# Three FFN1 tiles begun inside the attention of batch 0, and attention visits of three tiles throughout

## The chip, the cores and the metric

One NeuronCore of a Trainium2 chip runs the whole program; the other cores are idle. The metric is the device time of one execution in microseconds. The profiler gives the span from the first to the last instruction; in the executions listed below the time is the span plus 1.8 us. Where the text calls an execution slow, it is slower than its fellows. Batches, quads (groups of four heads; quad n belongs to batch n div 3) and FFN tiles are numbered from 0.

## The reference, cut to what matters

```python
# q, k, v: 8 batches x 12 heads x 448 x 64
scores = q @ k.T / sqrt(64) - log(448)
attn   = 1 / (1 + exp(-scores)) @ v          # sigmoid attention, no row sums
x      = attn.transpose(0, 2, 1, 3).reshape(3584, 768)
g      = x @ w_gate                          # 768 x 1536
out    = (g * sigmoid(g) * (x @ w_val)) @ w_out
```

A head needs no softmax sum, so TensorE and ScalarE (the sigmoid) can be interleaved freely with the FFN of an earlier batch.

## The kernel before

Attention of batch 0 runs first. After that the FFN of batch b is the main stream, and the attention of later batches is worked into it in "visits": a few QK tiles between two FFN units. A quad has seven QK tiles (`chunk(n, c)` or `qk_tile` + `sig_tile`), then one PV of 28 small matmuls. All PSUM is a ring of four tiles of two banks; every QK tile, PV, transposition, FFN1 tile and FFN2 tile takes the next one in turn and waits for its last user's readers. In the rows of the traces `pt` is the output of a sigmoid of the attention, `xT` the attention's result and FFN1's input (six tiles for a batch, one for each pair of heads), `hT` what FFN1's gate writes, and `T` a transposed q or k.

```python
ring = [psD.tile([128, 2, 512], FP32, ...) for i in range(4)]
class Banked:                       # takes the next tile of the ring
    def __init__(self, user=None):
        k = ring_at[0] % 4
        ring_at[0] += 1
        self.t = ring[k]
        ...
def qk_tile(n, c):                  # 4 matmuls of 64x64, 448 columns
    sc = Banked().t ...
def sig_tile(n, c, sc):             # ScalarE, 128 x 896
    nc.scalar.activation(out=pt, in_=sc[:, :, :S], func=SIGM, ...)
def pv(n, two=False):               # 28 matmuls, then 4 casts PSUM -> xT (VectorE)
    P = Banked().t ...
def ffn1(b, f):                     # 6 gate + 6 val matmuls, then the "gate":
    ...                             # ScalarE sigmoid, VectorE multiply, VectorE multiply
def ffn2(pb, m): ...                # 24 matmuls, then 2 copies

visits = [[(n, c) for c in cs] for n in range(NJ, NQ) for cs in (range(4), range(4, C))]
...
def attn_step(group, pvs):
    for part in (group[:2], group[2:]):
        scs = [(n, c, qk_tile(n, c)) for n, c in part]
        while pvs:
            pv(pvs.pop(0))
        for n, c, sc in scs:
            sig_tile(n, c, sc)
```

At the end of batch 0 two FFN1 tiles are begun while PV(2) is still to come: their first four input pairs (eight matmuls) need only PV(0) and PV(1).

```python
early = []
for f in range(2):
    Df = Banked("f")
    ffn1_mm(Df, 0, f, range(NP - 2))      # pairs 0..3
    early.append(Df)
    if f == 0:
        pv(2, two=True)
for f, Df in enumerate(early):
    ffn1_mm(Df, 0, f, range(NP - 2, NP))  # pairs 4, 5
    ffn1_gate(Df, 0, f)
```

## Time and profile before

| | before |
|---|---|
| median time of the first 3 runs | 434.53 us (434.45 to 435.88) |
| profiled execution | span 434.4 us, time 436.19 us, mean granted clock 0.995 |
| TensorE busy | 97% of the span |
| VectorE, ScalarE busy | 51%, 48% |
| visit of four QK tiles with PV | 2.48 us |
| visit of three QK tiles | 0.78 us |

The rows that the prediction rests on are printed in the prediction.

### The profile page before, as it was taken

How to read it: one execution, taken by the hardware profiler on the slowest of the kernel's cores; microseconds unless marked ns; L12 is line 12 of the kernel's file. 1: busy time of each engine (PE TensorE's matmuls, PEld its weight loads, DVE VectorE, ACT ScalarE, POOL GpSimd, SP SyncE). 2: the span in 40 equal slices, each digit the busy share in tenths (PEclk: the TensorE clock that was granted, in tenths of full speed). 3: DMA queues.
4: the chain of work that ended last, by engine and by line, in shares of the span. 5: the costliest groups of instructions: out<-in, count | busy, mean ns of one | idle time of the engine just before them, and what ended most of it. 6: DMA issues, size and time to landing. Idle time of an engine off the chain costs nothing.

```text
span 434.4 us, 7926 instructions
## 1 busy us (share of the span) xinstructions
PE 419.4 (97%) x3275; PEld 221.0 (51%) x3275; DVE 220.8 (51%) x366; ACT 208.0 (48%) x269; POOL 116.5 (27%) x166
## 2 busy tenths in 40 slices
PE   7789999999999999999999999999999999999995
PEld 2444554445555444544555544544555545555563
DVE  3645656546424656546424546555624456555322
ACT  3975885744523745745524545646533442222000
POOL 4563340730526455000426434400022100000000
PEclk9989999999999999999999999999999999999999
DMA  8999899999476997300386999720023400000234
GB/s 297 235 277 204 195 173 159 181 229 152 86 208 150 223 205 208 70 0 2 50 208 155 210 131 236 161 43 2 2 72 78 106 0 2 1 2 0 50 96 109
DMA packets 55940, 53.92 MB, mean 124 GB/s; under 512 B 33824, under 2 KB 50592, under 8 KB 55904
## 3 DMA queue, kind: packets, MB, share of 16 engines
q0 software_dynamic: 20896, 39.20, 41.7%
q1 hardware_dynamic: 34656, 13.67, 19.1%
q10 hardware_dynamic: 352, 0.56, 0.4%
q8 instruction: 25, 0.41, 0.4%
q14 instruction: 11, 0.09, 0.1%
HBM read 47.19 MB, written 11.01 MB: 134 GB/s over the span
## 4 chain that ended last, share of the span: by engine, by line
PE 81%; ACT 9%; DVE 6%; issue 3%; DMA 1%; DVEq 0%; ACTq 0%
PE ps_D L242 47%; PE ps_D L281 26%; ACT pt L202 7%; PE ps_D L191 5%; PE ps_D L214 2%; DVE hT L262 2%; DVE t L258 2%; DVE T L175 1%; DMA st<-in_q_dram 1%; DVE xT L229 1%; ACT s L256 1%; PE ps_D L167 1%; DVE c L145 0%; DVE oe L304 0%; ACT oe L300 0%
## 5 line engine op out<-in xcount | busy, mean ns | idle before, releaser
L202 ACT ACTIVATE pt<-ps_D,sb_t 128x896 f16<-128x896 f32 x168 | 156.3, 1007 | 93.4 <-PE ps_D L191 92.3
L242 PE MATMUL ps_D<-xT,wg 128*128 128x448 f16 x576 | 125.1, 353 | 2.0 <-ACT pt L202 0.4
L242 PE MATMUL ps_D<-xT,wv 128*128 128x448 f16 x576 | 125.0, 352 | 0.0
L281 PE MATMUL ps_D<-wo,hT 128*128 128x384 f16 x672 | 111.7, 326 | 0.8 <-ACT pt L202 0.4
L258 DVE TENSOR_TENSOR t<-ps_D,s 128x448 f16<-128x448 f32 x96 | 59.8, 623 | 87.9 <-ACT s L256 86.5
L256 ACT ACTIVATE s<-ps_D 128x448 f16<-128x448 f32 x96 | 52.5, 547 | 98.2 <-PE ps_D L242 96.8
L281 PEld LDWEIGHTS <-hT 128*128 128x128 f16 x672 | 65.2, 98 | 47.1 <-issue 4.6
L242 PEld LDWEIGHTS <-wg 128*128 128x128 f16 x576 | 54.8, 98 | 59.3 <-issue 11.6
L242 PEld LDWEIGHTS <-wv 128*128 128x128 f16 x576 | 56.4, 98 | 52.6
L229 DVE CAST xT<-ps_D 64x448 f16<-64x448 f32 x94 | 58.5, 622 | 29.5 <-PE ps_D L214 25.6
L311 DVE TENSOR_SCALAR osb<-ps_D 128x384 f32<-128x384 f32 x55 | 30.7, 558 | 71.5 <-PE ps_D L281 70.7
L262 DVE SCALAR_TENSOR_TENSOR hT<-ps_D,t 128x448 f16<-128x448 f32 x96 | 60.0, 625 | 10.4 <-DVE t L258 0.5
L321 POOL DMA_DIRECT2D out_dram<-osb x42 | 22.3, 536 | 143.6 <-DVE osb L311 143.6
L145 POOL CAST c<-st 128x896 bf16<-128x896 f32 x41 | 38.0, 936 | 75.6 <-issue 30.6
L191 PE MATMUL ps_D<-T,T 64*64 64x448 bf16 x672 | 48.1, 371 | 4.6 <-DVE T L175 1.9
L214 PE MATMUL ps_D<-pt,v 64*64 64x448 f16 x672 | 37.0, 357 | 0.5 <-ACT pt L202 0.5
L191 PEld LDWEIGHTS <-T 64*64 64x64 bf16 x672 | 16.3, 108 | 27.9 <-issue 19.3
L214 PEld LDWEIGHTS <-v 64*64 64x64 f16 x672 | 20.3, 109 | 13.8 <-issue 2.1
L136 POOL DMA_DIRECT2D v<-in_v_dram x24 | 17.7, 737 | 0.1
L131 POOL DMA_DIRECT2D st<-in_k_dram x20 | 14.7, 734 | 3.0 <-DVE c L145 3.0
L131 POOL DMA_DIRECT2D st<-in_q_dram x20 | 14.6, 732 | 0.6 <-DMA v<-in_v_dram 0.6
L300 ACT ACTIVATE oe<-ps_D 64x384 f32<-64x384 f32 x1 | 0.5, 484 | 27.9 <-PE ps_D L281 27.9
(21 smaller groups left out, 47.9 us busy)
## 6 DMA issues: line engine op xcount, KB each, us to landing
st<-in_q_dram POOLq DMA_DIRECT2D x20, 448.0 KB, 4.8
st<-in_k_dram POOLq DMA_DIRECT2D x20, 448.0 KB, 6.8
out_dram<-osb POOLq DMA_DIRECT2D x42, 192.0 KB, 3.1
v<-in_v_dram POOLq DMA_DIRECT2D x24, 224.0 KB, 8.0
wg<-in_moe_w_gate_dram POOLq DMA_DIRECT2D x4, 576.0 KB, 14.4
wv<-in_moe_w_val_dram POOLq DMA_DIRECT2D x4, 576.0 KB, 14.6
wo<-in_moe_w_out_dram POOLq DMA_DIRECT2D x4, 576.0 KB, 12.0
out_dram<-osb SPq DMA_DIRECT2D x12, 192.0 KB, 2.7
```

Source lines behind the costliest of these rows:

```text
L131: (eng or nc.sync).dma_start(out=st, in_=src_of(n, which))
L145: eng.tensor_copy(out=t.rearrange("p c h d -> p h c d"), in_=st.rearrange("p h (c d) -> p h c d", c=C)[:, :, lo:hi, :],)
L191: nc.tensor.matmul(out=sc[w * 64:(w + 1) * 64, h2, :S], lhsT=kt[r, w * 64:(w + 1) * 64], rhs=qt[r, :, w * 64:(w + 1) * 64], start=True, st ...
L202: nc.scalar.activation(out=pt, in_=sc[:, :, :S], func=SIGM, bias=sb_t, scale=qkscale)
L214: nc.tensor.matmul(out=P[h2 * 64:(h2 + 1) * 64, w, :S], lhsT=vt[r, h2, c * D:(c + 1) * D], rhs=pt[r, h2, :], start=(c == 0), stop=(c == C ...
L229: cp = nc.vector.tensor_copy(out=o, in_=i)
L242: nc.tensor.matmul(out=D.t[:, i, :S], lhsT=w16[f // FW][:, pr, cs], rhs=xT[(b, pr)], start=(pr == 0), stop=(pr == NP - 1),),
L256: D.read(nc.scalar.activation(out=s16, in_=D.t[:, 0, :S], func=SIGM), 0)
L258: D.read(nc.vector.tensor_tensor(out=t1, in0=D.t[:, 0, :S], in1=s16, op=MULT), 0)
L262: nc.vector.scalar_tensor_tensor(out=hT[(b // 2, f)][:, b % 2, :], in0=D.t[:, 1, :S], scalar=HSC, in1=t1, op0=MULT, op1=MULT),
L281: nc.tensor.matmul(out=D.t[:, half, :hw], lhsT=h[:, m * 128:(m + 1) * 128], rhs=wo16[f // FW][:, f % FW, half * hw:(half + 1) * hw], start ...
L311: nc.vector.tensor_scalar(out=osb[:, hs], in0=D.t[:, half, :hw], scalar1=HREC, scalar2=None, op0=MULT),
```

## The change

It wants to fill the attention of batch 0, where ScalarE sets the pace, with one more FFN1 tile, and to make the visits fit the ring: three QK tiles and a PV are four PSUM tiles.

```diff
 class Banked:
-    def __init__(self, user=None):
-        k = ring_at[0] % 4
-        ring_at[0] += 1
+    def __init__(self, user=None, at=None):      # 'at' chooses a ring place
+        if at is None:
+            at = ring_at[0] % 4
+            ring_at[0] += 1
+        k = ring_order[at]
 ...
-    visits = [[(n, c) for c in cs] for n in range(NJ, NQ) for cs in (range(4), range(4, C))]
+    tiles = [(n, c) for n in range(NJ, NQ) for c in range(C)]
+    visits = [tiles[i:i + 3] for i in range(0, len(tiles), 3)]
         if b == 1:
-            vtime.append(3 * FU1 + frac * (FIRST - 3 * FU1))
+            vtime.append(4 * FU1 + frac * (FIRST + 1.0 - 4 * FU1))
         else:
-            vtime.append(FIRST + 1.0 + (b - 2 + frac) * PER)
+            vtime.append(FIRST + 3.5 + (b - 2 + frac) * PER)
 ...  # casts of quad 3 right after those of quad 2; trans_pe(3) ahead of quad 2's QK tiles
+    chunk(2, 3)
+    chunk(2, 4)
+    k0 = ring_at[0] % 4
+    early = [Banked("f")]
+    for prs in (range(2), range(2, NP - 2)):
+        ffn1_mm(early[0], 0, 0, prs)
+    chunk(2, 5)
+    chunk(2, 6)
+    early.append(Banked("f"))
+    ffn1_mm(early[1], 0, 1, range(NP - 2))
+    pv(2, two=True, at=(k0 + 1) % 4)
+    early.append(Banked("f", at=(k0 + 2) % 4))
+    ffn1_mm(early[2], 0, 2, range(NP - 2))
     for f, Df in enumerate(early):
         ffn1_mm(Df, 0, f, range(NP - 2, NP))
         ffn1_gate(Df, 0, f)
+    ring_order[:] = [(k0 + 1 - i) % 4 for i in range(4)]
 ...  # the transpositions, loads and casts hung to a visit are now hung to a QK tile;
 ...  # 'while' over due visits became 'if': at most one visit per FFN unit
```

More of the change, by code (lines that the diff above doesn't have):

```diff
@@ L70 @@
     ring = [psD.tile([128, 2, 512], FP32, tag=f"D{i}", name=f"ps_D{i}") for i in range(4)]
+    ring_order = [0, 1, 2, 3]
     ring_at = [0]
@@ L203, in sig_tile, with pv @@
         pts[(n, c)] = pt
-    def pv(n, two=False):
+    def pv(n, two=False, at=None):
         b, j = divmod(n, NJ)
-        P = Banked().t
+        P = Banked(at=at).t
         vt = v16.pop(n)
@@ L331 @@
             for f in range(NF):
-                if (b, f) not in ((0, 0), (0, 1)):
+                if b or f > 2:
                     units.append((FU1, ffn1, (b, f)))
@@ L408 @@
     cast(2, 1, V)
+    cast(3, 0, V)
+    cast(3, 1, V)
     chunk(0, 5)
@@ L416 @@
     trans_pe(2)
-    cast(3, 0, V)
-    cast(3, 1, V)
     w_load("g", 1)
@@ L426 @@
     chunk(1, 6)
+    trans_pe(3)
     for c in range(3):
@@ L429 @@
     pv(1)
-    chunk(2, 3)
-    trans_pe(3)
     ready(4)
@@ L436 @@
     w_load("v", 3)
-    for c in range(4, C):
-        chunk(2, c)
-    early = []
-    for f in range(2):
-        Df = Banked("f")
-        ffn1_mm(Df, 0, f, range(NP - 2))
-        early.append(Df)
-        if f == 0:
-            pv(2, two=True)
+    chunk(2, 3)
[11 more added lines that the diff above has]
+    ffn1_mm(early[2], 0, 2, range(NP - 2))
     for f, Df in enumerate(early):
@@ L448 @@
         ffn1_gate(Df, 0, f)
-    begin = {(n, i): [] for n in range(NJ, NQ) for i in range(2)}
-    begin[(3, 1)] += [lambda: ready(5)]
-    begin[(4, 0)] += [lambda: fetch(6)]
-    begin[(4, 1)] += [lambda: ready(6)]
+    ring_order[:] = [(k0 + 1 - i) % 4 for i in range(4)]
+    ring_at[0] = 0
+    post = []
+    begin = {(n, c): [] for n in range(NJ, NQ) for c in (0, 4)}
+    begin[(3, 0)] += [lambda: post.append(4)]
+    begin[(3, 4)] += [lambda: ready(5)]
+    begin[(4, 0)] += [lambda: post.append(5), lambda: fetch(6)]
+    begin[(4, 4)] += [lambda: ready(6)]
     begin[(5, 0)] += [lambda: fetch(7)]
+    begin[(5, 4)] += [lambda: post.append(6)]
     begin[(6, 0)] += [lambda: ready(7), lambda: fetch(8)]
     begin[(7, 0)] += [lambda: ready(8), lambda: fetch(9)]
-    begin[(7, 1)] += [lambda: fetch(10)]
+    begin[(7, 4)] += [lambda: fetch(10)]
     begin[(8, 0)] += [lambda: ready(9), lambda: ready(10), lambda: fetch(11)]
-    for i, at in enumerate(((5, 1), (6, 1), (7, 0), (7, 1))):
+    for i, at in enumerate(((5, 4), (6, 4), (7, 0), (7, 4))):
         begin[at].append(lambda i=i: w_load("o", i))
@@ L466 @@
             begin[(n, 0)].append(lambda n=n: fetch(n + 3))
-    tcur = 2 * FU1
+    tcur = 3 * FU1
     vi = 0
-    pend, post = [], []
+    pend = []
     for dur, fn, args in units:
-        while vi < len(visits) and tcur >= vtime[vi]:
+        if vi < len(visits) and tcur >= vtime[vi]:
             group = visits[vi]
@@ L477 @@
             attn_step(group, pvs)
-            n, c = group[-1]
-            for act in begin[(n, int(c == C - 1))]:
-                act()
-            if c == C - 1:
-                pend.append(n)
-            elif n + 1 < NPE:
-                post.append(n + 1)
+            for n, c in group:
+                for act in begin.get((n, c), ()):
+                    act()
+                if c == C - 1:
+                    pend.append(n)
         if pend and (
```

## The prediction

> **What bounds the kernel now.** I read the page first (busy shares, the slices), then the waits of TensorE, then its timeline from end to end, because a group mean of 353 ns says nothing of the spacing.
>
> ```profile
> PE 419.4 (97%) x3275; PEld 221.0 (51%) x3275; DVE 220.8 (51%) x366; ACT 208.0 (48%) x269; POOL 116.5 (27%) x166
> ...
> PEclk9989999999999999999999999999999999999999
> ```
>
> TensorE is busy 97% of the span and no other engine is over half. But starts in the timeline show that matmuls overlap: six FFN1 matmuls take 1.135 us start to start (0.189 us each), a QK tile of four 64x64 matmuls 0.19, a PV of 28 takes 1.33, a transpose 0.062. I took (next start minus own start) minus these costs for every row. The excess is about 12 us before the first FFN1 tile at 28 us, 3.3 us between 36.5 and 69.2, some 10 us in the attention visits from there to 356 us, and nothing after. So three regions matter.
>
> Region one is the attention of batch 0, where ScalarE sets the pace: 21 sigmoids of 0.92 to 1.0 us run from 8.4 to 29.8 us, while TensorE has little to do and waits for buffers. These are rows of the whole timeline:
>
> ```profile
> 20.86 1.33 PE L191 MATMUL ps_D<-T,T 64*64 64x448 bf16 x12 [0.62 <-DVE T L175]
> 22.12 2.56 PE L214 MATMUL ps_D<-pt,v 64*64 64x448 f16 x28
> 24.80 2.53 DVE L229 CAST xT<-ps_D 64x448 f16<-64x448 f32 x4 [2.93 <-ACT pt L202]
> 24.81 0.95 PE L167 MATMUL ps_D<-idn,c 128*128 128x128 bf16 x14
> 27.39 0.57 PE L191 MATMUL ps_D<-T,T 64*64 64x448 bf16 x8 [1.31 <-DVE xT L229]
> 27.88 1.91 ACT L202 ACTIVATE pt<-ps_D,sb_t 128x896 f16<-128x896 f32 x2 [0.68 <-PE ps_D L191]
> ```
>
> The last two QK tiles of batch 0 need the PSUM tile that PV(1) used and wait 1.31 us until VectorE has taken PV(1) out; ScalarE is idle 0.68 us for them. PV(1) took 2.4 us where the others take 1.3: the windows view gives the clock there.
>
> ```profile
> 21.00:22.00 1.00, 1.00 (x12) 0.50 1.15 389
> 22.00:23.00 1.00, 1.00 (x16) 0.50 1.03 421
> 23.00:24.00 1.00, 1.00 (x20) 0.50 1.09 263
> ```
>
> Columns: stretch, its length, TensorE busy, granted clock, DMA share, GB/s. The clock is half from about 20.9 to 24.3 us.
>
> Region three is the visits: groups of QK tiles between FFN units. Two of them in TensorE's timeline, first with a PV, then without:
>
> ```profile
> 66.84 0.57 PE L191 MATMUL ps_D<-T,T 64*64 64x448 bf16 x8
> 67.24 1.49 PE L214 MATMUL ps_D<-pt,v 64*64 64x448 f16 x28
> 68.56 0.55 PE L191 MATMUL ps_D<-T,T 64*64 64x448 bf16 x8
> ...
> 173.11 0.76 PE L191 MATMUL ps_D<-T,T 64*64 64x448 bf16 x12
> 173.80 1.31 PE L242 MATMUL ps_D<-xT,wg 128*128 128x448 f16 x6
> ```
>
> FFN1's stream before them ends at 66.75 and 173.02 (last half begun plus 1.135), and FFN1 resumes at 69.23 and 173.80: the four-tile visit with PV costs 2.48 us, the three-tile one 0.78. Pure streaming would be 2.09 and 0.57. Both lose about 0.21 around the change of tile shape (0.09 going in, 0.12 coming out); the four-tile visit loses 0.18 more, because with PV it takes five of the four PSUM tiles, so its fifth user and the FFN1 after it wait for the first and second sigmoid (ScalarE starts them at 67.27, the second ends at about 69.13).
>
> **What the Trainium skill says.** "TensorEngine Tiling (Array Packing)", Key Properties: changing the tiling mode drains TensorE. The trace agrees: 0.09 + 0.12 us at each visit; so more visits cost more drains. "TensorE: Matmul & The Clock Gate", Part 1: the clock falls to half when a free-running window of about 3.4 us saw too little matmul activity, and the phase varies from run to run. The 3.4 us at 0.50 above fit that. "VectorE: DVE Perf Modes", the perf-mode tier table: a tensor_tensor with a PSUM operand has only the slowest mode. The trace has 623 ns for it and 622 for each fp32 cast of xT out of PSUM, so a PV leaves four casts, 2.53 us in a row. "Perfetto Trace Analysis", Identifying the Most-Contended Engine, warns that matmul busy share is a bad measure of headroom; hence my use of starts.
>
> **The change part by part.** No arithmetic is added or removed, only moved. I read the new instruction order and the PSUM tile of each step, and laid it down with the durations above.
>
> A. Batch 0. Quad 3's casts go to VectorE right after quad 2's, at 14.8 us (its loads land near 12.9; VectorE is idle then) and its transposes go to TensorE at 20.06, where it waits 0.62 us for quad 2's copies. QK(2,0..2) follow from 20.95, held by the sigmoids of their tiles' last users, to 22.2; PV(1) starts at about 22.25 as now. Then QK(2,3), (2,4), the first third of FFN1 tile 0, and QK(2,5), (2,6) after PV(1)'s casts.
> With full clock: PV(1) ends 23.57, its casts end 26.1; FFN1 tile 0 runs to 26.7, waiting for the fourth cast; QK(2,5), (2,6) to 27.1; last sigmoid ends 28.8 (now 29.8); tile 1's four pairs end 28.6, PV(2) 29.95, tile 2's four pairs 31.46, and the last two pairs of three tiles, 12 x 0.189 = 2.27, end at 33.7. Now the third tile ends at 36.5: gain 2.8 us.
> With the clock at half until 24.3: PV(1) ends 24.7, the casts 27.4, QK(2,6) 28.4, PV(2) 31.25, third tile 35.05: gain 1.45 us.
> Quad 3's transposes put 0.87 us of matmul into the window of 17.5 to 20.9 us, which had only about 1.5 us; I give 0.6 to the full clock.
>
> B. Batch 1 now has seven visits, one before each of FFN1 tiles 4 to 10, where there were six, with two transposes directly between FFN1 and a visit. Walking them, with sigmoids of 0.93, gates of two times 0.62 after a 0.55 sigmoid, and copies of 0.55: from the end of tile 2 to the end of tile 11 takes 32.6 us, of which 29.7 is streaming (9 FFN1 tiles 20.4, 21 QK 4.0, two PV 2.7, three transposes 2.6), 1.5 drains and about 1.4 waits for gates and copies. Before, the same work runs from 36.5 to 71.5 less one visit of quad 6 (2.48): 32.5. Even: -0.1 us.
> But the visit with PV(5) is shifted one unit later: in the new order PV(5) stands one QK tile ahead of batch 1's first FFN1 tile, which needs its xT; before, FFN1 tile 11 of batch 0 lay between. Casts begin 0.23 us after PV(5) ends and take 2.53, so the last xT comes at 2.76. FFN1 starts at about 0.3 and its sixth matmul is due at 1.25. TensorE waits 1.5 us, once. -1.5 us.
>
> C. Quads 6 to 23. Before: 18 pairs of visits at 2.48 + 0.78 = 3.26, 58.7 us. After: 42 visits of three at 0.78 and 18 PV at 1.33, 56.7 us, because three tiles and PV are just four PSUM tiles and nobody waits for a sigmoid. +2.0 us (3.1 from waits gone, less about 1.2 for six more visits' drains).
>
> The tail from 356 us is the same. Sum: 2.8 - 0.1 - 1.5 + 2.0 = 3.2 us with full clock, 1.9 with the half clock; weighted 2.7. From 434.5 that is 431.8; I take 431.6, as the walk of A leaves some slack that I counted in full.
>
> **The rivals.** (1) The gain of A is lost to waits in the denser batch 1: seven visits one FFN1 tile apart, with ScalarE at 3 x 0.93 + 0.55 = 3.3 us per visit against about 3.9 for TensorE. For it: the gates lag sigmoids there, and before had 0.44 to 0.64 us of excess at such visits. Against: ScalarE is not the longer one. It would give 433 to 434.5. (2) PV(5) does not stall FFN1, or batch 0 gains more: 429.5 to 430.3. Against: matmuls with pairs 4 and 5 carry waits on VectorE in the built order. (3) Weights come late: FFN1's first val weights land near 22 us in the trace, 2.5 us ahead of need; the second group's near 31.6, needed near 34.9. If the new loads of quad 5, issued some 3 us earlier, slowed them, 1 to 2 us would go. (4) The new clock window falls elsewhere and halves a dense FFN1 stretch: up to 1.7 us lost. (5) Three-tile visits with PV still wait, for the gate of the FFN1 tile just before, as the third QK takes its buffer: 18 x 0.2 = 3.6 us at most. Against: that gate ends some 0.9 us after its tile, and the third QK comes 1.7 us after.
>
> **Range and chances.** All large terms are small against 2% (8.7 us). Two clock states and the rivals span 429.6 to 433.6. Over 2% faster would need three times my sum: 0.03. Slower over 2%: 0.02.
>
> **What would show it right or wrong.** A: the last sigmoid of batch 0 ends near 28.8 and the third FFN1 tile near 33.7 (35.05 at half clock); the windows between 20 and 25 us show whether the clock fell. B: a wait of the first FFN1 tile of batch 1 on the xT casts, about 1.5 us in total, in TensorE's waits. C: visits with PV near 2.1 us instead of 2.48, those without at 0.78. I am wrong if PV visits stay at 2.4, if batch 1's visits lose over 0.4 us each, or if a weight load holds TensorE.

## More of the kernel before

The profiled execution was slower than each of the three runs. The trace of the kernel before is therefore a trace of a slow execution.

## The result, and the profile after

The changed kernel took 434.35 us (median of 6, 434.0 to 435.1) against 434.77 us (median of 6, 434.15 to 435.88) for the kernel before on the same chip. The ratio is 0.999 with a 95% interval of 0.9973 to 1.0006. (Ratios are the mean time of one kernel's fast runs over that of the other's of the same rounds, so not quite the ratio of the medians.) No difference clear of noise, where I had predicted 2.9 us.

The two traces, however, differ by 1.1 us (span 433.3 against 434.4). Where that comes from, region by region, taken from the starts of TensorE's rows in both traces:

| Stretch | before | after | gain |
|---|---|---|---|
| A: start of PV(0) to the end of the third FFN1 tile | 20.95 | 19.05 | +1.90 |
| B: from there to the end of batch 0's last FFN1 tile, without quad 6's visit | 32.61 | 33.32 | -0.71 |
| first FFN1 tile of batch 1 | 2.27 | 3.86 | -1.59 |
| C: quad 6's visits with PV(5) and on to PV(23), same work | | | +1.58 |

The last row is worked out so. From the end of that FFN1 tile to PV(23) it is 281.80 us before and 282.80 after, but the second contains one FFN1 tile (2.27) and one QK tile (0.19) more: 1.46 gained. The visit with PV(5) takes 2.48 before and 2.17 with one QK tile less after: 0.12 more. The sum of the rows is 1.18, and PV(0) starts 0.07 later in the trace after (15.53 instead of 15.46); the last FFN2 stream starts 1.12 us earlier (401.31 instead of 402.43), so the rows leave nothing over.

First the lines of region A after (times in us from the span's start, duration, engine, source line, tiles, count, idle time before and its releaser):

```profile
20.26 0.96 PE L170 MATMUL ps_D<-idn,c 128*128 128x128 bf16 x14
22.39 1.52 PE L217 MATMUL ps_D<-pt,v 64*64 64x448 f16 x28
23.95 2.55 DVE L232 CAST xT<-ps_D 64x448 f16<-64x448 f32 x4 [1.87 <-PE ps_D L217]
24.89 0.54 PE L245 MATMUL ps_D<-xT,wg 128*128 128x448 f16 x2 [0.51 <-ACT pt L205]
26.56 0.35 PE L245 MATMUL ps_D<-xT,wg 128*128 128x448 f16 x1 [0.56 <-DVE xT L232]
27.21 0.57 PE L194 MATMUL ps_D<-T,T 64*64 64x448 bf16 x8
27.70 1.90 ACT L205 ACTIVATE pt<-ps_D,sb_t 128x896 f16<-128x896 f32 x2 [1.06 <-issue]
```

PV(1) is at full speed (1.33 us to the next row's start), and the windows view confirms it: columns as in the prediction, the granted clock is the fifth figure.

```profile
21.00:22.00 1.00, 0.72 (x12) 1.00 1.17 388
22.00:23.00 1.00, 0.80 (x20) 1.00 1.02 406
23.00:24.00 1.00, 1.00 (x25) 1.00 1.11 279
```

Still, the last two sigmoids of batch 0 end at 29.6, not at 28.8 as I had them. The first FFN1 tile stops for the fourth cast of PV(1), ending at 26.5, and stands ahead of QK(2,5) and QK(2,6) in TensorE's order, so ScalarE is now idle for 1.06 us before their sigmoids. (That it waits for these tiles follows from the order and the times; the bracket says "issue", so the profile names no releaser.)

Then the first FFN1 tile of batch 1 in the trace after, in TensorE's timeline, and three rows of the list of waits (total, times, longest). The first row holds this tile's two waits, 0.30 and 0.95, and the 0.56 of batch 0's first tile; the others are waits for a gate in batch 1's visits:

```profile
68.04 0.57 PE L194 MATMUL ps_D<-T,T 64*64 64x448 bf16 x8
68.45 1.49 PE L217 MATMUL ps_D<-pt,v 64*64 64x448 f16 x28
69.77 0.36 PE L194 MATMUL ps_D<-T,T 64*64 64x448 bf16 x4
70.06 0.93 PE L245 MATMUL ps_D<-xT,wg 128*128 128x448 f16 x4
71.30 0.35 PE L245 MATMUL ps_D<-xT,wg 128*128 128x448 f16 x1 [0.30 <-DVE xT L232]
```

```profile
PE ps_D L245 <- DVE xT L232: 1.8, 3, 0.9
...
PE ps_D L217 <- DVE hT L265: 0.7, 1, 0.7
...
PE ps_D L194 <- DVE hT L265: 0.4, 1, 0.4
```

In the timeline four matmuls run, the fifth waits for the xT of pair 4 and the sixth, at 72.59, for that of pair 5. VectorE casts from 69.99 to 72.54.

A visit with PV further on shows what part C does. Compare it with the four-tile visit in the prediction:

```profile
88.00 1.30 PE L245 MATMUL ps_D<-xT,wv 128*128 128x448 f16 x6
89.23 0.57 PE L194 MATMUL ps_D<-T,T 64*64 64x448 bf16 x8
89.63 1.50 PE L217 MATMUL ps_D<-pt,v 64*64 64x448 f16 x28
90.95 0.36 PE L194 MATMUL ps_D<-T,T 64*64 64x448 bf16 x4
91.24 1.31 PE L245 MATMUL ps_D<-xT,wg 128*128 128x448 f16 x6
```

FFN1's stream ends at 88.00 + 1.135 = 89.13 and resumes at 91.24: 2.11 us. Nothing waits for a sigmoid.

So of the predicted mechanisms the trace shows the stall and the cheaper visits, at nearly the sizes given. What doesn't fit is the total: the traces differ by 1.1 us, the medians by 0.4.

### The profile page after: what moved, and what is told of

It reads as the page before. It is cut to its first block, busy times and chain, and to the rows that moved or that the text cites. A ratio compares the mean times of both kernels' runs of the same rounds, so it can differ in the third digit from the quotient of the medians.

```text
span 433.3 us, 7921 instructions
## 1 busy us (share of the span) xinstructions
PE 418.9 (97%) x3275; PEld 218.1 (50%) x3275; DVE 220.6 (51%) x366; ACT 209.9 (48%) x269; POOL 116.4 (27%) x166
## 4 chain that ended last, share of the span: by engine, by line
PE 91%; DVE 4%; ACT 3%; DMA 1%; issue 1%; DVEq 0%; ACTq 0%
PE ps_D L245 49%; PE ps_D L284 26%; PE ps_D L194 8%; PE ps_D L217 7%; ACT pt L205 2%; DVE xT L232 2%; DMA st<-in_q_dram 1%; PE ps_D L170 1%; DVE T L178 1%; DVE t L261 1%; DVE hT L265 1%; ACT s L259 0%; DVE c L148 0%; DVE oe L307 0%; ACT oe L303 0%
## 5 line engine op out<-in xcount | busy, mean ns | idle before, releaser
L245 PEld LDWEIGHTS <-wg 128*128 128x128 f16 x576 | 53.5, 98 | 59.6 <-issue 14.0
L314 DVE TENSOR_SCALAR osb<-ps_D 128x384 f32<-128x384 f32 x55 | 30.6, 557 | 72.9 <-PE ps_D L284 72.7
L217 PE MATMUL ps_D<-pt,v 64*64 64x448 f16 x672 | 36.0, 350 | 1.2 <-DVE hT L265 0.7
## 6 DMA issues: line engine op xcount, KB each, us to landing
wo<-in_moe_w_out_dram POOLq DMA_DIRECT2D x4, 576.0 KB, 15.3
```

Source lines behind the costliest of these rows:

```text
L217: nc.tensor.matmul(out=P[h2 * 64:(h2 + 1) * 64, w, :S], lhsT=vt[r, h2, c * D:(c + 1) * D], rhs=pt[r, h2, :], start=(c == 0), stop=(c == C ...
L245: nc.tensor.matmul(out=D.t[:, i, :S], lhsT=w16[f // FW][:, pr, cs], rhs=xT[(b, pr)], start=(pr == 0), stop=(pr == NP - 1),),
L314: nc.vector.tensor_scalar(out=osb[:, hs], in0=D.t[:, half, :hw], scalar1=HREC, scalar2=None, op0=MULT),
```

## The experiments

Theory 1: the trace of the kernel before was an untypical execution. It contains a stretch at half clock on the path (20.9 to 24.3 us), its time of 436.19 is 1.4 us over the kernel's median, and much of A's gain is the absence of that stretch, which most executions of the kernel before don't have either. Rival 2: the half clock belongs to the kernel before, and the change removes it. The other runs take the parts of the change apart. All kernels gave the right result. The medians come from six executions each, the kernel before has eleven in each of the three series. The series ran on different chips (the kernel before has medians of 435.21, 435.13 and 434.78 there), so two variants of different series are compared through their ratios to the kernel before, or region by region in their traces.

### before_copy: the kernel before again

No edit.

> The kernel before, unchanged, as a second look. Theory 1 (my baseline trace was an atypical execution: a stretch at half clock from 20.9 to 24.3 us cost it about 1.4 us, and time less span is 1.8 us, so that the median of 434.8 belongs to a span near 433.0): most executions have spans of 432.5 to 433.5, and a trace without half clock in 20 to 25 us ends batch 0's second FFN1 tile near 32.7 instead of 34.1. Rival 2 (the half clock is the rule for this kernel): spans near 434.4 with clock 0.995 in most executions, and the trace shows the half clock at about 21 to 24 us again.

Measured: 434.65 us (434.31 to 436.06), ratio 0.9991 (0.9965 to 1.0017); the profiled execution has a span of 432.6 us. Its windows and timeline:

```profile
10.00:12.00 2.00, 1.89 (x18) 0.58 1.05 371
12.00:14.00 2.00, 2.00 (x22) 0.57 1.29 206
20.00:21.00 1.00, 0.76 (x12) 1.00 1.29 208
21.00:22.00 1.00, 0.66 (x16) 1.00 1.14 412
22.00:23.00 1.00, 1.00 (x24) 1.00 1.03 414
23.00:24.00 1.00, 0.91 (x18) 1.00 1.12 247
```

```profile
21.34 1.52 PE L214 MATMUL ps_D<-pt,v 64*64 64x448 f16 x28 [0.50 <-ACT pt L202]
22.97 2.52 DVE L229 CAST xT<-ps_D 64x448 f16<-64x448 f32 x4 [1.88 <-PE ps_D L214]
25.55 0.57 PE L191 MATMUL ps_D<-T,T 64*64 64x448 bf16 x8 [1.13 <-DVE xT L229]
26.04 1.91 ACT L202 ACTIVATE pt<-ps_D,sb_t 128x896 f16<-128x896 f32 x2 [0.26 <-PE ps_D L191]
```

The same program has its half-clock stretch at 10 to 14 us here, where ScalarE's chain is not held up by it (ScalarE is busy all of these 4 us), and none at 21 to 24. The second early tile ends at 32.3 (34.1 in the first trace). Region A takes 14.67 to 34.57, 19.90 us instead of 20.95. So 1.05 us of A's 1.90 is the half clock of one execution, and theory 1 holds; the kernel before has no fixed half clock for the change to remove. All traces together say so more firmly. Of the five with the old batch 0 only the first has half clock on the way from PV(0) to the third tile's end, beyond a remnant at its start: A takes 20.95 there, 20.14 in visits_from_quad6, whose half clock ends at 15.4, and 19.89 to 19.90 in the other three. Of the nine with the new batch 0 eight take 19.04 or 19.05, and pv5_earlier, where the half clock ends at 15.3, takes 19.35. A is worth 0.85 us.

Against this second trace the table's sum is 0.85 - 0.71 - 1.59 + 1.58, which is 0.1 us. From PV(0) to the last FFN2 stream the whole stretch takes 385.94 us in it and 385.78 after. The other 0.79 us between the two traces of the kernel before lie ahead of PV(0), which starts at 15.46 and at 14.67. The executions agree if they are sorted by the granted clock listed with each (my sorting, after the fact). At 1.000 the kernel before has a median of 435.21 (nine executions) and the changed one 435.0 (four); at 0.996 434.26 (nine) and 434.09 (three); at 0.989 to 0.991 434.65 (eight) and 434.47 (five). That is 0.2 us each time, and it shows how much of the spread comes with the clock.

### early_only: part A alone

```diff
 # the changed kernel, with the visits and their hooks of the kernel before
-    visits = [tiles[i:i + 3] for i in range(0, len(tiles), 3)]
+    visits = [[(n, c) for c in cs] for n in range(NJ, NQ) for cs in (range(4), range(4, C))]
-            vtime.append(FIRST + 3.5 + (b - 2 + frac) * PER)
+            vtime.append(FIRST + 1.0 + (b - 2 + frac) * PER)
```

> Part A alone (third early FFN1 tile, chosen PSUM tiles, quad 3's transposes moved up; visits of four and three as before). Theory 1: at full clock A is worth only 0.5 to 1.0 us, so the ratio to before is 0.998. Rival 2: A is worth the 2.0 us that the two traces show, ratio 0.9955. Rival 3 (A's gain is lost again in batch 1 because the gates of three tiles come at once): ratio 1.000, and the trace shows over 4 us of waits of TensorE between the third tile and batch 0's last one.

Measured: 434.06 us (433.64 to 434.85) against 435.21, ratio 0.9974 (0.9949 to 0.9999). In the trace A takes 14.42 to 33.45, 19.03 us: the same 0.87 below the second trace of before. Region B takes 33.12 instead of 32.62, because the gates of three early tiles now end one after another, and the last two QK tiles of the first visit of four wait for them (that visit's QK tiles take 2.03 us of TensorE against 1.54). Theory 1 has A's size right (0.85 us, not the 2.0 of rival 2, which the times alone would not exclude), but more than half of it is lost again as rival 3 had it: 0.85 - 0.50 leaves some 0.35 us.

### visits_from_quad6: part C alone

```diff
 # the kernel before, with
-    visits = [[(n, c) for c in cs] for n in range(NJ, NQ) for cs in (range(4), range(4, C))]
+    visits = [[(n, c) for c in cs] for n in range(NJ, 2 * NJ) for cs in (range(4), range(4, C))]
+    rest = [(n, c) for n in range(2 * NJ, NQ) for c in range(C)]
+    visits += [rest[i:i + 3] for i in range(0, len(rest), 3)]
```

> Part C alone: visits of three tiles from quad 6 on, everything before that as in the kernel before. By my sum 18 PV visits lose 0.37 us each and six more visits cost 0.2 each: 2.0 us faster, ratio 0.9955; in the trace PV visits take 2.11 instead of 2.48. Rival: the medians show next to nothing (ratio over 0.998) because what is saved in the visits is given back elsewhere, such as at visits just before FFN2.

Measured: 433.09 us (432.66 to 433.74) against 435.21, ratio 0.995 (0.9923 to 0.9976): 2.1 us, the predicted 2.0. Against the second trace of the kernel before, its own trace gains 1.85 us from batch 0's third tile on. Part C keeps its gain when it stands alone.

### pv5_earlier: the changed kernel without the stall

```diff
 # the changed kernel, with
-            vtime.append(FIRST + 3.5 + (b - 2 + frac) * PER)
+            vtime.append(FIRST + 1.0 + (b - 2 + frac) * PER)
-    begin[(5, 4)] += [lambda: post.append(6)]
+    begin[(5, 0)] += [lambda: post.append(6)]
```

> The changed kernel with quad 6's visits one unit earlier, so that PV(5) again stands one FFN1 tile ahead of batch 1's first FFN1 tile (and quad 6's transposes two visits earlier to be ready). Theory: the 1.6 us wait for the xT casts in the changed kernel goes, ratio to before 0.995 to 0.996 where the changed kernel has 0.999. Rival: the denser order in front of it turns it into a new wait (quad 6's transposes or the buffers), ratio stays above 0.998.

Measured: 433.68 us (433.2 to 434.04), ratio 0.9961 (0.9937 to 0.9985), where the changed kernel has 0.999. The first FFN1 tile of batch 1 takes 2.27 us again, so the stall is gone, and by the medians 1.1 of its 1.6 us come back. The ratio is just above the expected 0.995 to 0.996, and its interval does not quite exclude the rival's 0.998. The trace shows a part of the rival: quad 6's transposition moved before a visit with PV, and that visit now waits (its two QK tiles ahead of the PV take 1.18 us of TensorE instead of 0.40).

### quad6_pv5_late: the stall alone

```diff
 # visits_from_quad6, with
-            vtime.append(FIRST + 1.0 + (b - 2 + frac) * PER)
+            vtime.append(FIRST + 3.5 + (b - 2 + frac) * PER)
```

> Visits of three from quad 6 on, but quad 6's visits start 2.5 us later as in the changed kernel, so that PV(5) stands directly ahead of batch 1's first FFN1 tile; nothing else. Theory: TensorE waits 1.5 to 1.6 us for the last xT cast there, ratio rises from 0.995 to 0.9985, and the trace shows the wait at the fifth and sixth matmul of that tile. Rival: the wait only displaces later ones, ratio stays below 0.9965.

Measured: 434.65 us (434.23 to 435.13), ratio 0.9994 (0.998 to 1.0008), against 433.09 and 0.995 without the shift (in another series; the intervals do not overlap): 1.6 us. TensorE's timeline shows the wait where it was put:

```profile
69.96 0.93 PE L242 MATMUL ps_D<-xT,wg 128*128 128x448 f16 x4
71.19 0.35 PE L242 MATMUL ps_D<-xT,wg 128*128 128x448 f16 x1 [0.30 <-DVE xT L229]
72.49 0.35 PE L242 MATMUL ps_D<-xT,wg 128*128 128x448 f16 x1 [0.95 <-DVE xT L229]
72.68 1.29 PE L242 MATMUL ps_D<-xT,wv 128*128 128x448 f16 x6
```

The sixth matmul starts 2.53 us after the first; undisturbed it would be 0.95. So one visit set one FFN1 tile too late takes back three quarters of what 42 better visits gain.

### visits_only: the denser batch 1

```diff
 # the kernel before up to the end of batch 0's attention, with the changed kernel's visits, and
-            vtime.append(FIRST + 3.5 + (b - 2 + frac) * PER)
+            vtime.append(FIRST + 1.0 + (b - 2 + frac) * PER)
```

> Visits of three tiles throughout, with batch 0's attention as in the kernel before and PV(5) one FFN1 tile ahead of batch 1. Against the version with such visits from quad 6 on (ratio 0.995) it differs only in batch 1's quads 3 to 5. Theory: seven denser visits lose there about 0.9 us more than six of four and three, because a QK tile takes the buffer of the FFN1 tile just before, whose gate stands behind three sigmoids on ScalarE: ratio 0.997. Rival: batch 1's visits gain like all others, ratio 0.994 to 0.995.

Measured: 433.97 us (432.94 to 435.07), ratio 0.9978 (0.9959 to 0.9997), against 0.995 with the old visits in batch 1. The difference between the two medians is 0.9 us, as the theory had it, but the executions spread over 2.1 us and the two intervals overlap, so the times alone don't settle it. The traces do: from the third tile's end to batch 0's last, the same work takes 35.49 us here and 34.74 in visits_from_quad6. Two waits for a gate stand there, 0.69 us of idle time each, at 39.43 and 47.44. The changed kernel's trace has them in the same two places and is used to show them. Three engines around the visit at 41 us:

```profile
40.06 0.55 ACT L259 ACTIVATE s<-ps_D 128x448 f16<-128x448 f32 x1
40.20 0.94 PE L170 MATMUL ps_D<-idn,c 128*128 128x128 bf16 x14
40.65 0.62 DVE L261 TENSOR_TENSOR t<-ps_D,s 128x448 f16<-128x448 f32 x1 [2.05 <-ACT s L259]
41.07 0.57 PE L194 MATMUL ps_D<-T,T 64*64 64x448 bf16 x8
41.38 0.62 DVE L265 SCALAR_TENSOR_TENSOR hT<-ps_D,t 128x448 f16<-128x448 f32 x1
42.05 0.38 PE L194 MATMUL ps_D<-T,T 64*64 64x448 bf16 x4 [0.41 <-DVE hT L265]
```

The FFN1 tile ahead of this visit ended at 40.2. Its gate matmuls were done more than 1 us earlier, but its sigmoid came on ScalarE after the three sigmoids of the visit before (37.38 to 40.06), so its gate ended only at 42.0. With a single FFN1 tile between visits and a transposition in the ring, the third QK tile gets just that buffer. PV(3) meets the same at 48.8 and loses 0.9 us.

### early_and_quad6: A and C without the two losses

```diff
 # early_only, with the visits of visits_from_quad6
```

> Parts A and C together, batch 1 with visits of four and three and PV(5) one FFN1 tile ahead: the change without the two losses. If the parts add up: early part alone 0.9974 and visits from quad 6 alone 0.995 give 0.9925 (432.0 us where before is 435.2). Rival: A's gain is absorbed again by batch 1, ratio 0.995 as without A.

Measured: 432.45 us (432.03 to 434.23) against 435.13, ratio 0.9942 (0.9927 to 0.9957). My sum is missed: by the medians A alone (1.15 us) and C alone (2.1) should give 3.3 us, and the two together give 2.7; the expected 0.9925 lies just outside the interval, and the rival's 0.995 inside. By the ratio A contributes 0.0008, which is the 0.35 us that early_only's trace leaves of it. One execution of six, the profiled one, took 434.23. TensorE's timeline of it:

```profile
90.99 0.57 PE L194 MATMUL ps_D<-T,T 64*64 64x448 bf16 x8
92.95 0.38 PE L194 MATMUL ps_D<-T,T 64*64 64x448 bf16 x4 [1.39 <-DMA T<-c]
```

QK(8,0) waits for quad 8's DMA transpose. Visits of three bring the first tiles of a quad up to two tiles forward, and visits that start 2.5 us earlier do so again; the changed kernel's shift by 2.5 us, which caused the stall at PV(5), gives room here.

### early_quad6_dma: transposes of quads 4 to 6 by DMA

```diff
 # early_and_quad6, with
-    NPE = 2 * NJ + 1
+    NPE = NJ + 1
```

> Parts A and C together, and quads 4 to 6 transposed by DMA like all later quads: TensorE loses three times 14 transposes (0.87 us each, 2.6 us) and VectorE six copies, so batch 1's visits no longer wait for those. If the DMA transposes land in time: ratio 0.986 to 0.988 (about 429.5 us). Rival: the DMA engines are busy with weights until about 50 us, the transposes land late and TensorE waits for quad 4 or 5; ratio over 0.9925.

Measured: 437.77 us (435.26 to 439.88), ratio 1.006 (1.0031 to 1.0088). My theory fell. The two longest waits of TensorE are new:

```profile
PE ps_D L194 <- DMA T<-c: 3.9, 1, 3.9
PE ps_D L245 <- DMA wv<-in_moe_w_val_dram: 1.6, 1, 1.6
```

A transpose (quad 6's, at 67.7 us) and a weight come late. These 5.5 us exceed the 2.6 us of transpositions removed, but leave 2.4 of the distance of 5.3 us to early_and_quad6 in the medians. The clock accounts for them: during the wait it fell to half, from 66.1 to 72.9 us.

```profile
66.00:68.00 2.00, 0.28 (x4) 0.52 1.30 208
68.00:70.00 2.00, 2.00 (x28) 0.50 1.15 205
```

From 67.7 to 73.4 two QK tiles, a PV, a QK tile and half an FFN1 tile take 5.66 us. The same pieces take about 3.15 at full clock, so 2.5 us are lost, and 5.5 - 2.6 + 2.5 is 5.4 us. That is one trace of one execution; the other five were not traced.

### after_copy: the changed kernel again

No edit.

> The changed kernel again, for a second trace and five more rounds beside the others. If its parts are what the single runs showed (early part -0.5 to -1.1 us, visits from quad 6 on -2.1, denser batch 1 +0.9, PV(5) directly ahead of FFN1 +1.6), the sum is -0.1 to -0.7 us: ratio 0.9985 to 1.000. A ratio below 0.9965 would mean that something in the parts does not add up.

Measured: 434.54 us (434.0 to 435.14) against 434.78, ratio 0.9984 (0.9959 to 1.0009). In this trace A takes 14.90 to 33.94, 19.04 us, as in the first trace after; B takes 33.32 and the first FFN1 tile of batch 1 3.86 us, all as in the first trace after. In the traces the parts add up; the ratio stands at the edge of the expected range, and its interval alone would not exclude 0.9965.

### split_first, first_visit_early and first_early_split: mending what is left

```diff
 # split_first = early_and_quad6, with quad 3 in visits of 2, 3 and 2
+              ((range(2), range(2, 5), range(5, C)) if n == NJ else (range(4), range(4, C)))]
 # first_visit_early = early_and_quad6, with only PV(5)'s visit early
-            vtime.append(FIRST + 1.0 + (b - 2 + frac) * PER)
+            vtime.append(FIRST + (1.0 if grp[0] == (2 * NJ, 0) else 3.5) + (b - 2 + frac) * PER)
 # first_early_split = both
```

> Early part and visits of three from quad 6 on (432.45 us, 0.9942), with quad 3's visits split 2, 3, 2. In those traces the first visit of four after the three early FFN1 tiles loses 1.15 us on its last two QK tiles, which wait for the gates of the second and third early tile; a first visit of two needs only the first two buffers. Theory: 0.5 to 0.9 us less than without the split (one more visit costs 0.2), ratio 0.9925. Rival: the wait only moves to the next FFN1 tile, ratio stays 0.994.

Measured: 431.5 us (430.85 to 435.06) against 434.78, ratio 0.9927 (0.9893 to 0.996). Five of six executions are below 432. The ratio's interval does not exclude the rival; the trace does, as from the third tile's end to batch 0's last it takes 34.12 us instead of 35.28. The profiled execution has 435.06 and a wait of 2.45 us for a DMA transpose, now quad 7's:

```profile
80.34 0.57 PE L194 MATMUL ps_D<-T,T 64*64 64x448 bf16 x8 [2.45 <-DMA T<-c]
```

About 1 us after this wait the clock fell to half, from 81.3 to 84.7 us. The FFN1 tile there takes 3.96 us instead of 2.27: the 1.7 us of the prediction's fourth rival, in this variant.

> Early part and visits of three from quad 6 on, where only the visit with PV(5) comes early and all later visits come 2.5 us later, as in the changed kernel. One slow execution of the version with all visits early (434.2) had a wait of 1.4 us for quad 8's DMA transpose, at 91 us. Theory: with later visits that wait doesn't occur and PV(5) still causes none: median 432.2 to 432.5 and no execution over 433.3. Rival: the slow execution was clock or chance; spread as before.

Measured: 432.92 us (432.19 to 433.45), ratio 0.9946 (0.992 to 0.9971). The median is a little above what I had expected. No wait for a transpose is in its trace.

> Both of the last two mends together: if they add, 431.6 to 431.9 us, ratio 0.992, the fastest version here. Rival: no better than either alone.

Measured: 431.62 us (431.18 to 432.07) against 434.78, ratio 0.9915 (0.9888 to 0.9942), the best ratio, with a spread of 0.9 us. Its median is not below that of split_first; what the second mend brings is that no execution is slow. This version beats the kernel before and the changed one by about 3 us; it is the change with both losses mended. That the early visits caused the two slow executions is supported (in these four versions two of twelve executions with early visits, each with the wait in its trace, and none of twelve with the later ones), not proved. Both were the profiled, first execution of their run, so being first or profiled may have a part in it. Of the other versions with early visits, visits_from_quad6 and pv5_earlier had no slow execution in twelve, and visits_only had two that were not traced.

## Why the prediction was wrong, point by point

**A, predicted +2.8 at full clock (1.45 at half, weighted to about 2.3), measured +0.85 against a comparable execution.** This is the step that failed. Two terms were mis-sized. First, I subtracted the walk at full clock from a trace at half clock and gave that 0.6. But the reference is the median execution of the kernel before, and of the five traces with its batch 0 four have no such stretch at 21 to 24 us: 1.05 us of the 2.8 was not there to gain. I had quoted the page on the free-running window, that the phase varies from run to run, and applied it to the kernel after only. (The forecast for the kernel after was right: none of the nine traces with the new batch 0 has half clock there.) The sign to see was in the result: the profiled execution took 436.19 us, the runs 434.45 to 435.88. Second, the walk itself was 0.9 us too fast (third tile at 34.58 instead of 33.7): PV(1) started 0.14 late and its casts began 0.24 us after it, not at once, and I left out the drains at each change between FFN1 and 64x64 tiles, 0.08 to 0.13 each, four times, though I had measured them for the visits. 2.8 - 1.05 - 0.9 is the 0.85 measured. A small slip of reading besides: the third tile ends at 36.41 before, and 36.5 is where the next QK tile starts.

**B, predicted even (-0.1), measured -0.7.** I had waits for gates and copies of 1.4 us in the walk, but underrated how late one ends when its sigmoid stands behind three others, and missed that PV(3) would take such a buffer (0.9 us at 48.8). That was my first rival, which I set aside with the argument that ScalarE's load per visit is below TensorE's. Load was the wrong measure: what counts is how long a buffer is held. (I also took 0.062 us for a transpose. The trace has 0.056; the 0.87 us for fourteen includes the 0.09 of the change to 64x64 tiles, which I counted again among the drains.)

**The stall of the first FFN1 tile of batch 1, predicted -1.5, measured -1.59** in the trace and 1.6 us in the isolated experiment. Right in place, cause and size.

**C, predicted +2.0, measured 2.1 us** by itself (1.85 in its trace) and 1.58 in the traces of the full change, where one visit just ahead of FFN2 loses 0.33. A visit with PV takes 2.11 us as predicted, and one without 0.78 (0.79 in the trace after). Rival 5, that the third QK tile waits for the gate before it, occurs in batch 1 and not in general.

**Weights and clock (rivals 3 and 4)**: no wait for a weight is in either trace of the changed kernel, and no half clock falls into a dense stretch of FFN1. Rival 4 did occur in split_first, after a wait for a DMA transpose.

So the sum should have read 0.85 - 0.7 - 1.5 + 2.0, some 0.6 us. That the change would stay within 2% was right, the 2.9 us were not.

## What to carry to other kernels

Before subtracting a walk from a trace, compare the profiled execution's time with the median of the runs: if it is slower by more than the effect looked for, get a second trace. An interleaving that must hit fixed buffers should be checked for which buffer each tile gets and how long the last reader of that buffer is behind, not only for the load of each engine. Split a change into its parts on the chip: here losses of 0.7 and 1.6 us hid nearly all of the gain, and with both mended the kernel is 3.2 us faster than before (431.62 against 434.78).

## What the Trainium skill lacked or had wrong

- "TensorEngine Tiling (Array Packing)", Key Properties, says that changing the tiling mode drains TensorE and gives no figure. Here it costs 0.09 us going from 128-row tiles to 64x64 tiles and 0.12 us coming back, the same at dozens of visits.
- "TensorE: Matmul & The Clock Gate", Part 1, has the fall to half clock after an idle window of about 3.4 us. Here the clock fell at 20.9 us though TensorE was busy in the profile for 1.70 of the 3.41 us before (17.47 to 20.88) and never idle for more than 0.62 us at a time. The page gives no busy share at which the clock falls, also not where it has short pauses do it ("A second HAM failure mode"). I cut all fourteen traces, up to 424 us, into stretches of 3.41 us counted from their clock records. The clock fell after twelve, in which TensorE was busy 0.29 to 0.54 of the time, and after no other; the lowest shares without a fall are 0.52 and 0.58. Between 14 and 30 us the lowest share is 0.50 to 0.64 in the five traces with the old batch 0, and 0.65 to 0.73 in the nine with the new one.
- The page calls the loss of a cold start under 1% of a typical span, and that holds: the place of the half clock in batch 0 moved the span by 1.05 us, 0.24%. But it is more than the effect under study.
- No page says that a granted clock of 1.00 can mean "nothing recorded". In the first traces of both kernels the windows view gives 1.00 from the start on, but the packed traces hold no clock record before 14.05 us (before) and 13.86 us (after), and the view counts what is missing as full clock. The durations say half: eight QK matmuls at 7.8 us take 0.96 us, against 0.57 in the second trace of before, and fourteen transposes at 11.3 take 1.68 against 0.94 later on.
- No page that I used gives the spread of a DMA transpose's landing. In the same region of similar programs TensorE waited 1.4 us and 2.45 us for one in single executions, and not at all in others.
